# A tuned attention and feed-forward kernel: the differences of the weights' two parts move from VectorE to GpSimd

## The chip, the cores and the metric

The kernel runs on one core of a Trainium2 chip. The metric is the device time of one launch in microseconds (us); the kernel before was run three times, and the median counts. A core has five instruction queues that matter here: TensorE (PE in the profile; PEld is its loading of stationary operands), VectorE (DVE), ScalarE (ACT), GpSimd (POOL) and SyncE (SP), which in this kernel issues all DMAs. Each engine works through its own queue in order; semaphores tie the queues together.

## The reference

Four batches of eight heads run a gated recurrence over 768 steps, and its output goes through a feed-forward layer with a squared ReLU:

```
state = alpha[t][:, None] * state + outer(k[t], v[t])      # per batch and head, 48 x 48
y[t]  = q[t] @ state
x     = y, batches and steps as rows, heads side by side   # 3072 x 384
out   = square(maximum(x @ w_in, 0)) @ w_out               # w_in 384 x 2048, w_out 2048 x 384
```

All tensors are fp32 for the reference; the weights arrive as 64-bit floats, which the kernel turns into fp32 itself.

## The kernel before

**Staging.** The recurrence is cut into blocks of 128 steps: 6 per batch, 24 in all. Four blocks make a group of 512 rows, and there are six groups (0 to 5). TensorE works through the feed-forward layer of group after group, and the recurrence of the groups to come is woven between its matmuls. Blocks need ScalarE (logarithm, exponentials, copies from PSUM) and VectorE (scaling of q and k, masks, states).

**Two parts for each operand.** The first matrix in group 0, three quarters of the second in group 0 and half of it in group 1 run as plain fp32 matmuls (`ffn_in` L901, `out_plain` L817). Everywhere else each operand is split: `b` is a rounded upper part of the weight w, `l` the scaled rest of it, and `d` the difference `b - l`; the activations get parts `a`, `l`, `d` in the same way. Three passes of faster matmuls (`b` with `a`, `l` with `l`, `d` with `d`) then replace one plain product. In the layer's first matrix these are `in_x` (passes b and l, L726) and `in_y` (pass d, L737); in the second `out_x` (L826) and `out_y` (L846).

**Making the weights' parts.** w_in and w_out are cut into eight pieces each ("i0" to "i7", "o0" to "o7" below), of 128 partitions by 768 numbers. Each piece goes through four steps: `cast_w` (ScalarE makes `b`, L646), `rest_w` (VectorE makes `w - b`, through `combine`, L641), `scale_w` (ScalarE scales it to `l`, L660, and stores it to DRAM), and `diff_w` (VectorE makes `d = b - l`, through the same helper, so also L641, and stores it to DRAM with `keep`, L651). `prepare` (L675) places the four steps 1.6 units of matmul work apart; the order in which the sixteen pieces come is i1, o6, i0, o7, i2 to i7, o4, o5, o0 to o3. They are made once, between 105 us and 209 us of the span, under the end of group 0 and in group 1. Later groups load `l` and `d` again from DRAM (`pump`, L680, DMA at L684), in the order in which TensorE will use them, as far as the pool of 26 tiles has room.

**Order.** The order on each engine is the order in which the program emits the steps: the list of words in `AT` up to the first full layer, and from there `weave` (L1041), which emits units of matmul work and drops events between them as their due time comes. Nothing is reordered afterwards.

**The queue of GpSimd.** It clears tiles and makes constants in the first 6.2 us of the span. After that it has held only twelve semaphore instructions, one for each pair of blocks: `passed = nc.gpsimd.nop(...)` (L511, L550) waits for a matmul of the recurrence on TensorE, and TensorE waits for it before the second half of that pair's products, `yb` (L394). That is how the program makes TensorE wait for its own earlier matmuls.

**VectorE in the stretch that the change touches.** Beside the steps above it splits the activations of the second matrix (`hl`, L641, and `hd`, L695, out of `ha`, which ScalarE makes at L691) and those of the first (`xl` L641, `xd` L695, out of `xa`), squares and adds (`hid` L641, L750), scales q and k (L299), splits logarithms (L270, L271), makes masks and states (L425, L455, L471, L472), and adds partial outputs (`osb` L838 and L641).

Of the kernel before, what the change touches and what calls it, by code (L numbers as in the profile page):

```python
# [13 lines left out]
ALU = mybir.AluOpType  # L14
# [11 lines left out]
def kernel(  # L26
# [12 lines left out]
    nc = tc.nc  # L39
# [44 lines left out]
    def wt(name, dt=FP32, shape=(KM, DF // NW)):  # L84
        return wt_pool.tile([128, *shape], dt, tag="wt", name=name)
# [553 lines left out]
    def combine(steps):  # L639
        for o, x, op, z in steps:  # L640
            nc.vector.tensor_tensor(out=o, in0=x, in1=z, op=op)  # L641
# [8 lines left out]
    def keep(x, w, p):  # L650
        nc.sync.dma_start(out=kept_parts[x, w, p], in_=words(made[x, w, p]))  # L651
        stored.add((x, w, p))
# [10 lines left out]
    def diff_w(w, p):  # L663
        b, l = here["b", w, p].bitcast(FP32), made["l", w, p].bitcast(FP32)
        d = made["d", w, p] = wt("wd", FP32R, shapes[w])
        cut.add((w, p))
        combine(((d, b, ALU.subtract, l),))
        keep("d", w, p)
        for x in "ld":
            t = made.pop((x, w, p))  # L670
            if w == "i" or p >= NW - AT["k0"] or (x == "l" and p >= NW - AT["k1"]):
                here[x, w, p] = t
        pump()

    def prepare(at, w, p):  # L675
        step = AT["wstep"]
        fs = (cast_w, rest_w, scale_w, diff_w)
        return [(at + i * step, f, (w, p)) for i, f in enumerate(fs)]

    def pump():  # L680
        while todo and todo[0] in stored and len(here) + len(made) + 2 * NW - len(cut) < room[0]:
            key = todo.pop(0)
            here[key] = wt("w" + key[0], FP32R, shapes[key[1]])
            nc.sync.dma_start(out=words(here[key]), in_=kept_parts[key])  # L684
# [476 lines left out]
```

## Time and profile before

| | |
|---|---|
| runs | 528.08, 524.81 and 525.77 us; median 525.77 us |
| the profiled execution | 526.04 us, of which the span is 524.3 us |
| VectorE busy | 363.8 us (69%), 631 instructions |
| ScalarE busy | 314.8 us (60%) |
| GpSimd busy | 5.3 us (1%), 29 instructions |
| granted TensorE clock | 1.00 over the whole span |
| DMA | 102.36 MB, mean 195 GB/s |

The profiled execution is 0.27 us above the median and spends 1.74 us outside its span. The view of groups gives the busy time of a kind of instruction, the mean duration of one, and what ended the engine's idle time before it. The view of waits gives, for each kind of instruction, the total time that its engine stood idle for it and what released it. The chain that ended last is followed back from the last instruction; its rows are a start, a length and what ran. Rows of the timeline are a start, a duration, the engine and line, and what is written from what.

### The profile page before, as it was taken

What the parts mean: (1) busy time and instruction counts of PE and PEld (TensorE: products, weight loads), DVE (VectorE), ACT (ScalarE), POOL (GpSimd) and SP (SyncE); (2) the same over time, 40 slices, a digit from 0 to 9 for tenths busy, and PEclk for the clock granted to TensorE, in tenths of its full rate; (3) what the DMA queues carried; (4) which work ended last, traced back from release to release, by engine and by line L of the source; (5) the groups of instructions that cost most, each with busy time, mean ns of one, the idle gap of its engine ahead of it and who ended that gap; (6) DMA issues with size and microseconds to landing.
All of it is one profiled execution on the core that took longest, in us unless ns stands there. A gap on an engine that the chain in (4) does not pass through costs nothing.

```text
span 524.3 us, 13198 instructions
## 1 busy us (share of the span) xinstructions
PE 510.0 (97%) x5340; PEld 420.3 (80%) x5340; DVE 363.8 (69%) x631; ACT 314.8 (60%) x662; POOL 5.3 (1%) x29
## 2 busy tenths in 40 slices
PE   7899999998999999889999999999999999999997
PEld 5675446668888669768899988899988899988997
DVE  4778979898879579755697465697365485363861
ACT  3668893688899566456963266963265773164620
POOL 4000000000000000000000000000000000000000
PEclk9999999999999999999999999999999999999999
DMA  9989778235689576998885697864674444798201
GB/s 184 203 266 221 206 209 212 44 91 228 211 214 222 141 228 169 278 330 219 200 208 184 207 285 181 220 194 144 222 262 143 159 149 138 252 352 296 78 0 61
DMA packets 139324, 102.36 MB, mean 195 GB/s; under 512 B 109808, under 2 KB 112896, under 8 KB 139264
## 3 DMA queue, kind: packets, MB, share of 16 engines
q1 hardware_dynamic: 139264, 101.52, 67.6%
q8 instruction: 43, 0.70, 0.6%
q14 instruction: 17, 0.14, 0.1%
HBM read 84.17 MB, written 17.33 MB: 194 GB/s over the span
## 4 chain that ended last, share of the span: by engine, by line
PE 76%; ACT 9%; DVE 7%; DMA 4%; SPq 2%; issue 2%; POOLq 0%; DVEq 0%
PE o L801 33%; PE h L718 31%; PE y L394 4%; ACT power L177 2%; DMA a_in<-in_alpha_dram 2%; PE sckv L414 2%; PE T L571 2%; PE sckv L442 2%; SPq L119 1%; DMA wd<-di 1%; DMA v_in<-in_v_dram 1%; DVE w_out L192 1%; DVE w_out L195 1%; ACT r L917 1%; ACT x L609 1%
## 5 line engine op out<-in xcount | busy, mean ns | idle before, releaser
L718 PE MATMUL h<-xd,wd 128*128 128x512 f32 x240 | 66.8, 393 | 3.5 <-ACT ha L691 1.9
L718 PE MATMUL h<-xa,wb 128*128 128x512 f32 x240 | 68.9, 395 | 0.0
L718 PE MATMUL h<-xl,wl 128*128 128x512 f32 x240 | 67.8, 391 | 0.0
L641 DVE TENSOR_TENSOR hid<-h,hid 128x512 f32<-128x512 f32 x40 | 27.5, 689 | 46.2 <-PE h L718 43.4
L735 ACT ACTIVATE h<-h 128x512 f32<-128x512 f32 x40 | 23.3, 582 | 59.1 <-PE h L718 58.9
L609 ACT COPY x<-y 32x256 f32<-32x256 f32 (+2 forms) x132 | 47.2, 365 | 17.6 <-PE y L394 12.8
L801 PE MATMUL o<-wd,hd 128*128 128x384 f32 x304 | 53.8, 334 | 1.4 <-DVE osb L838 1.4
L718 PEld LDWEIGHTS h<-xd,wd 128*128 128x128 f32 x240 | 44.4, 188 | 13.2 <-ACT ha L691 2.3
L801 PE MATMUL o<-wb,ha 128*128 128x384 f32 x160 | 54.2, 338 | 0.0
L801 PEld LDWEIGHTS o<-wd,hd 128*128 128x128 f32 x304 | 52.7, 188 | 1.7 <-DVE osb L838 1.7
L801 PE MATMUL o<-w_out,hid 128*128 128x384 f32 x160 | 53.5, 490 | 0.0
L801 PE MATMUL o<-wl,hl 128*128 128x384 f32 x160 | 53.5, 335 | 0.0
L718 PEld LDWEIGHTS h<-xl,wl 128*128 128x128 f32 x240 | 45.1, 188 | 10.0 <-DVE xl L641 0.3
L718 PEld LDWEIGHTS h<-xa,wb 128*128 128x128 f32 x240 | 44.3, 188 | 9.2
L801 PE MATMUL o<-wb,hx 128*128 128x384 f32 x144 | 48.7, 338 | 0.0
L801 PE MATMUL o<-wl,hx 128*128 128x384 f32 x144 | 48.1, 334 | 0.0
L801 PEld LDWEIGHTS o<-w_out,hid 128*128 128x128 f32 x160 | 29.9, 190 | 19.7
L911 PE MATMUL h<-x,w_in 128*128 128x512 f32 (+1 forms) x120 | 43.6, 513 | 0.5 <-ACT x L609 0.5
L733 ACT ACTIVATE hid<-h 128x512 f32<-128x512 f32 x40 | 24.3, 607 | 29.2 <-PE h L718 29.1
L691 ACT ACTIVATE ha<-hid 128x512 fp32r<-128x512 f32 x40 | 25.5, 636 | 23.8 <-DVE hx L641 12.9
L911 PEld LDWEIGHTS h<-x,w_in 128*128 128x128 f32 x120 | 22.1, 190 | 18.2 <-issue 14.1
L641 DVE TENSOR_TENSOR hl<-hid,ha 128x512 fp32r<-128x512 f32 x40 | 27.4, 686 | 12.0 <-ACT ha L691 12.0
(117 smaller groups left out, 880.0 us busy)
## 6 DMA issues: line engine op xcount, KB each, us to landing
wd<-do SPq DMA_DIRECT2D x36, 384.0 KB, 3.1
wl<-lo SPq DMA_DIRECT2D x34, 384.0 KB, 5.1
wl<-li SPq DMA_DIRECT2D x32, 384.0 KB
wd<-di SPq DMA_DIRECT2D x32, 384.0 KB, 5.1
raw<-in_moe_w_in_dram SPq DMA_DIRECT2D x8, 768.0 KB, 6.2
raw<-in_moe_w_out_dram SPq DMA_DIRECT2D x8, 768.0 KB, 4.8
v_in<-in_v_dram SPq DMA_DIRECT2D x24, 192.0 KB, 4.9
out_dram<-osb SPq DMA_DIRECT2D x24, 192.0 KB, 2.1
```

The costliest lines, as they stand in the source:

```text
L177: nc.scalar.activation(out=power, in_=power, func=AF.Relu, scale=2.0**23, bias=rebias)
L394: ins = nc.tensor.matmul(out=ys[e][64 * half : 64 * half + D + G * e, m % 2, p // 2, t], lhsT=lhsT, rhs=rhs, start=(half, e) not in seen, ...
L414: nc.tensor.matmul(out=ps[e][HALF[h], 0, p, :], lhsT=ks[rows, p, HALF[h]], rhs=qs[rows, p, HALF[h]], start=True, stop=True, skip_group_che ...
L442: nc.tensor.matmul(out=ps[h][64 * e : 64 * (e + 1), 1, p, G:64], lhsT=tile_of("k", n)[HALF[h], 2 * p + e, :], rhs=tiles["v"][n % NV][HALF[ ...
L609: copy(out=x[kk][to : to + m, t : t + 2], in_=blk[n]["y"][e][r : r + m, :, p // 2],)
L641: nc.vector.tensor_tensor(out=o, in0=x, in1=z, op=op)
L691: nc.scalar.activation(out=a, in_=x, func=AF.Copy, scale=NEAR)
L718: nc.tensor.matmul(out=acc["h", j], lhsT=here[w, "i", p][:, kk, jj * 128 : (jj + 1) * 128], rhs=x_parts[x][:, kk], start=start and kk == 0 ...
L733: nc.scalar.activation(out=hid[j], in_=x, func=AF.Copy, scale=E)
L735: nc.scalar.activation(out=x, in_=x, func=AF.Copy, scale=1.0 + E)
L801: nc.tensor.matmul(out=acc[t][:, 0:DM], lhsT=lhs[:, t * C : (t + 1) * C], rhs=rhs, start=start, stop=stop, skip_group_check=True,)
L911: nc.tensor.matmul(out=ps, lhsT=w[:, kk, c0 : c0 + 128], rhs=xT[g][kk][:, cols], start=(kk == 0), stop=(kk == KM - 1),)
```

## The change

One line of `diff_w` changes its engine. The subtraction has the same operands, sizes and types (128 x 768, two fp32 inputs in SBUF, one output in SBUF); it no longer goes through `combine`, so its line becomes L667. The semaphores follow the new engine.

```diff
     def diff_w(w, p):
         b, l = here["b", w, p].bitcast(FP32), made["l", w, p].bitcast(FP32)
         d = made["d", w, p] = wt("wd", FP32R, shapes[w])
         cut.add((w, p))
-        combine(((d, b, ALU.subtract, l),))
+        nc.gpsimd.tensor_tensor(out=d, in0=b, in1=l, op=ALU.subtract)
         keep("d", w, p)
```

The built program shows what moves: sixteen TensorTensor instructions leave VectorE's queue and stand in GpSimd's, behind its constants and between its semaphore instructions; the order of everything else on TensorE, VectorE, ScalarE and SyncE is the same. In GpSimd's queue the pieces stand between the semaphore instructions as: i1, o6, i0, the fourth semaphore instruction, o7, i2 to i7, the fifth, o4, o5, o0, o1, the sixth, o2, o3.

## The prediction

> **What bounds the kernel now.** I read the page first. TensorE is busy almost throughout, so work taken off VectorE pays only where TensorE stands idle.
>
> ```profile
> span 524.3 us, 13198 instructions
> PE 510.0 (97%) x5340; PEld 420.3 (80%) x5340; DVE 363.8 (69%) x631; ACT 314.8 (60%) x662; POOL 5.3 (1%) x29
> ```
>
> The view of the wd tiles gives what is moved: sixteen subtractions of 0.95 us between 115.7 and 207.2 us. They are the only rows that change their engine.
>
> ```profile
> L641 DVE TENSOR_TENSOR wd<-wb,wl x16: 949/951/959, 115.7 to 207.2; 128x768 fp32r<-128x768 f32 x16
> ```
>
> Then the view of waits, for TensorE alone (us in total, times, longest). Those after 104 us are these three; the idle rest lies ahead of 50 us and in the last 4 us, out of reach of the change.
>
> ```profile
> PE h L718 <- ACT ha L691: 1.9, 1, 1.9
> PE h L718 <- DMA wd<-di: 1.6, 1, 1.6
> PE o L801 <- DVE osb L838: 1.4, 1, 1.4
> ```
>
> The busy time by stretch (us, PE, PEld, DVE, ACT, POOL) says where VectorE matters: from 104 to 126 us VectorE (20.15 of 22) and ScalarE are as full as TensorE; from 128 to 215 us TensorE is never idle and VectorE has 15 us free.
>
> ```profile
> 104.00:126.00 22.00, 20.64 (x290) 14.94 (x289) 20.15 (x33) 19.43 (x41) 0.00 (x0) 1.00 0.50 166
> 128.00:215.00 87.00, 87.00 (x1050) 69.72 (x1049) 71.98 (x128) 65.10 (x137) 0.00 (x0) 1.00 0.73 202
> ```
>
> The chain that ended last shows which subtractions lie on the path in the first stretch (start, length, what):
>
> ```profile
> 115.77 0.87 DVE wd L641
> 116.63 0.87 DVE wl L641
> 117.50 0.61 DVE hl L641
> 118.12 0.02 issue
> 118.14 0.69 DVE hd L695
> 118.83 0.88 DVE wl L641
> 119.73 0.85 ACT wl L660
> ...
> 123.66 0.87 DVE wd L641
> 124.53 0.87 DVE wl L641
> 125.40 0.48 DVE osb L838
> ```
>
> Two of sixteen. The other fourteen run beside TensorE's work.
>
> **Part 1: what VectorE gains.** Each subtraction holds VectorE for 0.87 us from start to start; sixteen make 13.9 us, of which almost all was covered. At 115.77 the piece i1 goes, but hl behind it waits for ha on ScalarE, which ends at 116.55 + 0.61 = 117.16: hl starts at 117.2 and not 117.42, a gain of 0.2 us. The same 0.2 us is handed to wl at 119.73 and along ScalarE's queue, which runs without a gap from there (osb, wb, ha, 4.35 us of copies of x, wl, xa) until xa ends at 129.0. At 123.66 the piece o7 goes: osb L838 could start 0.9 us earlier, near 124.5 when TensorE's last sums are done, and out_y with it. But the matmuls of group 1 behind out_y need xa and xl, and xl follows xa, which came only 0.2 us earlier. So 1.36 us of idle time at 125.9 mostly comes back as a wait for xl, and the gain is 0.2 to 0.4 us; I take 0.3.
>
> **Part 2: what one subtraction costs GpSimd.** The rows of before hold no two-operand instruction on GpSimd. The nearest are a memset and a cast of 128x128 (start, duration):
>
> ```profile
> 2.85 0.20 POOL masks.py:197 MEMSET ident<- 128x128 f32 x1
> 4.00 0.29 POOL L217 CAST causal_r<-causal 128x128 fp32r<-128x128 f32 x1
> ```
>
> With memsets of 128x256 at 310 ns a memset costs 106 ns for each further 128 numbers. At that slope the cast grows to 0.29 + 5 x 0.106 = 0.82 us for 768 numbers, and that is the lower end; six whole casts, 1.73 us, are the upper one. A second operand has to be read as well, so I take 1.7 us, near the upper row. The Trainium skill gives 4,497 ns for such an operation on 2048 numbers ("GPSIMD Engine Reference", 3.1), by proportion an estimate of 1.69 us; no row here shows it.
>
> **Part 3: are the differences late?** On GpSimd they wait only for l from ScalarE (L660), no longer for VectorE's queue. i6 has its l at 153.87 + 0.84 = 154.7, so it ends near 156.4; VectorE ended it at 159.94, and TensorE uses it at 163.96. i7: l at 161.7, end 163.4, used after 166.2. o6 and o7 end near 118.3 and 122.3, wanted at 125.9. All have 2.8 us to spare or more, so a length of 1.7 us costs nothing. The DMAs that store d follow on SyncE, in their old places; SyncE waited 25 us in all for them, with loads behind, and none of those loads kept an engine waiting before 215 us. ScalarE's wb and VectorE's wl now wait for earlier GpSimd pieces at eight places, always one finished 5 us before. In GpSimd's queue o7, o4 and o2 stand behind semaphore instructions that wait for TensorE; of these only o4 meets one that is late (l at 169.1, the recurrence's matmuls done at 170.9), and it still ends at 172.6, against 172.85 on VectorE.
>
> **Part 4: the hold.** GpSimd and VectorE now read SBUF operands at the same time, which no row of before shows. The nearest rows are VectorE's own: a cast of 128x384 (L270) takes 0.35 us, a two-operand product of the same size (L299) 0.55. Reading is what its two-operand instructions are short of, so if GpSimd's reads come out of the same supply, the two hold each other up. At the one end that costs nothing; at the other each piece stops one VectorE instruction for 1.7 us. I take one hold for each piece that meets a waiting hl or xl, with VectorE passing first between its own back-to-back instructions:
> o6 (l ready at 116.64) runs to 118.3, hl starts there and not at 117.42, and wl and ScalarE's queue come 0.9 us later; xa begins at 128.24. i2 (l ready at 128.33) runs to 130.0, holds the first xl from 128.9, and the third xl ends at 131.9 and not 129.9. TensorE's group 1 starts 2.0 us later, and this includes part 1.
> The Trainium skill makes a rule of it: a VectorE instruction with two SBUF inputs and a GpSimd one that reads SBUF share a read interface, and whichever comes second is blocked for the whole instruction ("SBUF — State Buffer", Who interferes with whom). By the rule the sum is the slower one, without it the faster one below.
> Between 128 and 215 us VectorE sheds 11 x 0.87 = 9.6 us and is held for at most 11 x 1.7 = 18.7 us; with its 15 us free the load fits, and only a late release of a PSUM bank or of k and q before a transpose can show: 0 to 1.5 us, taken as 0.3.
>
> **Part 5: the reload at 222 us.** The stores of o2 and o3 (SyncE, 207.33) open a stretch in which the DMA engines are full (0.98 from 215 to 232 us), and the loads of d in it are what TensorE waits for: 1.6 us at 222.4 for di0; the 1.9 us at 229.35, put down to ha, end with the load of di1 that was issued at 219.91, for the matmuls wait for it too. l of o2 and o3 is ready at 203.3 and 204.1, but VectorE reached them only at 206.35, behind masks and states. On GpSimd they end at 205.1 and 206.8 if nothing holds them: the second store goes 1.4 us earlier, and the two waits of 3.5 us shrink by up to as much. With hd of 203.95 meeting GpSimd I take half, 0.7 us.
>
> **Sum**, against the profiled execution of 526.04 us: + 2.0 + 0.3 - 0.7 = + 1.6, so 527.6; that execution lies 0.27 us over the median, so 527.4 us.
>
> **The rivals.**
> *No hold.* The engines do not disturb each other: -0.3 and -1.4, so 525.77 - 1.7 = 524.1 us. For it: no row shows a hold. Against it: VectorE's 0.35 and 0.55 us.
> *GpSimd wins every gap.* A piece that is ready slips in at each dependent pair, too. i1 (l ready 108.87) holds hl at 109.69 for 1.7 us, 0.66 of it idle anyway: 1.0. o6 0.9. i0 goes between hl and hd: 1.7. o7 stops hl at 123: 0.8. i2 1.2. Together 5.6, with 1.0 us of bank stalls behind and no gain at 222 us, since hd goes after o2: 525.77 + 6.6 - 0.3 = 532.1 us, slower by more than 1%. It decides once the holds on the path pass 5.3 us in sum.
> *The semaphore queue.* Behind i0 on GpSimd stands the semaphore instruction that TensorE's yb waits for; yb started at 120.85. If that instruction goes only when i0 is finished, and i0 is held by hd and wl until 120.5, it comes at 122.2. The copies of x on ScalarE wait for yb: with its 0.7 us they start at 122.9, not 122.23 + 0.9, so ScalarE hides it, but out_x behind yb is 1.4 us late and out_y with it: + 1.4 on top, 528.8 us. For it: a queue works in order. Against it: i0 may end at 120.1.
>
> **How the numbers follow.** Forecast 0.45, no hold 0.26, every gap 0.19, the semaphore queue 0.10. A measurement of this kernel can tell about 1%, 5.3 us, from no change. Forecast, no hold and semaphore queue all lie within it; every gap lies above; 0.01 is left for faster, since TensorE's idle time within reach is under 5 us. The forecast's own range is 525.5 to 529.5. The range goes down to 523.8, 0.3 us under no hold, for a subtraction nearer to 0.82 us that lets the reload start earlier still, and up to 531.5, which leaves out most of every gap.
>
> **What would show it.** Sixteen rows on L667 of 1.4 to 2.0 us. VectorE's hl, hd and xl beside them longer than 0.69 us or starting after a piece ends (hold), or at 0.69 as before (no hold). The first matmul of group 1, at 128.8 before, near 130.8. yb right after i0's end would show the semaphore queue. The waits for di0 and di1 at 222 and 229 us shorter in sum than 3.5. The forecast is wrong if a wait for POOL appears on TensorE's L718 or L801, or if pieces take over 3 us each.

## The result

The changed kernel takes 532.22 us (median of 4 runs, 532.05 to 533.45), the kernel before 525.29 us (median of 4, 524.73 to 528.08): a ratio of 1.0124 with a 95% interval of 1.0094 to 1.0154. It is slower by some 6.5 us by that ratio (6.9 us between the medians), above the forecast of 527.4 us and above the end of the range at 531.5 us; the rival in which GpSimd wins every gap had 532.1 us. The profiled execution of after took 532.26 us, at a granted clock of 1.00.

The page of after, for the two lines that were shown of before:

```profile
span 530.5 us, 13220 instructions
PE 513.6 (97%) x5340; PEld 420.1 (79%) x5340; DVE 367.7 (69%) x615; ACT 315.2 (59%) x662; POOL 37.6 (7%) x45
```

VectorE lost sixteen instructions, and it is busy for 3.9 us longer than before. Matched one by one between the two traces, the instructions that stayed grew by 17.4 us in sum, 1.1 us for each piece; nearly all of it lies in thirteen of them, which grew by 0.8 to 1.6 us each. GpSimd is busy for 32.3 us more.

The view of the wd tiles gives the moved rows, now on GpSimd (durations in ns: least, median, most):

```profile
L667 POOL TENSOR_TENSOR wd<-wb,wl x16: 1830/1867/2496, 108.5 to 213.3; 128x768 fp32r<-128x768 f32 x16
```

The view of waits for TensorE (us in total, times, longest), the rows in the reach of the change:

```profile
PE h L718 <- ACT ha L691: 1.7, 1, 1.7
PE o L801 <- ACT wl L660: 1.3, 1, 1.3
PE cs L284 <- DVE lo L271: 1.2, 1, 1.2
...
PE o L801 <- DVE osb L838: 0.7, 1, 0.7
PE T L571 <- DVE k_in L299: 0.6, 1, 0.6
PE o L801 <- ACT osb L824: 0.5, 1, 0.5
...
PE cs L283 <- DVE hi L270: 0.5, 1, 0.5
PE h L718 <- DVE xl L641: 0.4, 1, 0.4
PE o L801 <- DVE hl L641: 0.4, 1, 0.4
```

No row names GpSimd: no difference is late. Instead there are waits for VectorE and for ScalarE's steps behind it, and one of the two waits at the reload, that for di0, is gone.

The busy time by stretch (us, PE, PEld, DVE, ACT, POOL), at the two places shown of before:

```profile
104.00:126.00 22.00, 19.77 (x281) 13.35 (x279) 18.55 (x24) 16.13 (x33) 8.42 (x4) 1.00 0.47 154
128.00:215.00 87.00, 83.76 (x957) 63.92 (x957) 69.29 (x105) 62.47 (x129) 23.23 (x12) 1.00 0.66 179
```

TensorE was busy for 20.64 us of the first and for all of the second; it now stands idle for 2.2 and 3.2 us. VectorE's instructions have a mean of 0.77 us (18.55 / 24) for 0.61, and of 0.66 us for 0.56: it does fewer of them and saves little time.

The chain that ended last runs through the held instructions (start, length, what):

```profile
108.40 0.96 DVE w_out L195
109.36 2.23 DVE hl L641
...
117.66 1.92 DVE hl L641
119.57 0.02 issue
119.60 2.22 DVE hd L695
121.81 0.88 DVE wl L641
...
129.59 0.85 ACT wl L660
130.44 0.53 ACT xa L691
130.97 0.02 issue
130.99 3.13 DVE xl L641 x3
134.12 0.04 issue
134.16 1.89 PE h L718 x7
```

Before, hl and hd on this chain took 0.61 and 0.69 us. The row of the first hl in the timeline of before (start, duration, row):

```profile
109.69 0.69 DVE L641 TENSOR_TENSOR hl<-hid,ha 128x512 fp32r<-128x512 f32 x1
```

To see what runs beside these instructions, here is the timeline of after, GpSimd first and then VectorE (in square brackets, the engine's idle time before the row and what ended it):

```profile
108.53 2.50 POOL L667 TENSOR_TENSOR wd<-wb,wl 128x768 fp32r<-128x768 f32 x1 [102.34 <-ACT wl L660]
117.18 4.08 POOL L667 TENSOR_TENSOR wd<-wb,wl 128x768 fp32r<-128x768 f32 x2 [6.15 <-ACT wl L660]
```

```profile
108.40 0.96 DVE L195 TENSOR_TENSOR w_out<-w_out,power 128x768 f32<-128x768 f32 x1
109.27 2.31 DVE L641 TENSOR_TENSOR hl<-hid,ha 128x512 fp32r<-128x512 f32 x1
...
117.66 1.91 DVE L641 TENSOR_TENSOR hl<-hid,ha 128x512 fp32r<-128x512 f32 x1 [0.56 <-ACT ha L691]
119.60 2.22 DVE L695 SCALAR_TENSOR_TENSOR hd<-ha,hl 128x512 fp32r<-128x512 f32 x1
```

The row of GpSimd's i1 begins at 108.53, while L195 runs: the piece is admitted, which means that it has all it waits for and stands at the head of its queue. It ends at 111.03. Less 1.83 us, the least of the sixteen durations, it began to work at 109.20, when L195 came to its end. hl stood in VectorE's queue right behind L195 and had nothing left to wait for, yet it ends at 111.58, 0.55 us after the piece. So GpSimd got in between two back-to-back instructions of VectorE, and 1.62 of the 1.83 us of its work show up as a longer hl. At 119.6 the same happens between hl and the hd that depends on it (i0, the second of the pair of pieces).

**Where the 6.2 us of span came from.** The timelines of the kernels are cut at the same instructions: S1 from the first hl (109.69 before) to the first matmul of group 1 with xd; S2 and S3 from there to two transposes of k (163.36 and 194.08); S4 on to the first matmul of group 2 (216.49); S5 the reload, to the next transposes (232.27); S6 to the start of the last matmuls with xd (485.24). Lengths in us:

| kernel | S1 | S2 | S3 | S4 | S5 | S6 |
|---|---|---|---|---|---|---|
| before | 23.37 | 30.30 | 30.72 | 22.41 | 15.78 | 252.97 |
| after | 27.99 | 32.19 | 32.44 | 22.99 | 13.74 | 252.83 |
| after less before | +4.62 | +1.89 | +1.72 | +0.58 | -2.04 | -0.14 |

The sum is +6.6; the first hl came 0.4 us earlier in after, a start that differs between executions of one kernel, too (109.69 and 110.81 us in two executions of the kernel before). Each part has its own place, so each can be tried alone.

### The profile page after: what moved, and what is told of

Read it like the earlier page. It is cut to its first block, busy times and chain, and to the rows that moved or that the text cites. A ratio compares the mean times of both kernels' runs of the same rounds, so it can differ in the third digit from the quotient of the medians.

```text
span 530.5 us, 13220 instructions
## 1 busy us (share of the span) xinstructions
PE 513.6 (97%) x5340; PEld 420.1 (79%) x5340; DVE 367.7 (69%) x615; ACT 315.2 (59%) x662; POOL 37.6 (7%) x45
## 4 chain that ended last, share of the span: by engine, by line
PE 78%; DVE 11%; ACT 5%; issue 2%; DMA 2%; SPq 1%; DVEq 0%; POOLq 0%; ACTq 0%
PE o L801 30%; PE h L718 29%; PE h L911 7%; PE y L394 3%; PE T L571 2%; PE sckv L414 2%; ACT x L609 2%; PE sckv L442 2%; DVE hl L641 1%; DVE wl L641 1%; DVE hd L695 1%; DMA v_in<-in_v_dram 1%; SPq L119 1%; DVE w_out L195 1%; DVE w_out L192 1%
## 5 line engine op out<-in xcount | busy, mean ns | idle before, releaser
L667 POOL TENSOR_TENSOR wd<-wb,wl 128x768 fp32r<-128x768 f32 x16 | 32.2, 2020 | 177.2 <-ACT wl L660 164.4
L641 DVE TENSOR_TENSOR hl<-hid,ha 128x512 fp32r<-128x512 f32 x40 | 31.6, 791 | 13.6 <-ACT ha L691 13.6
L691 ACT ACTIVATE ha<-hid 128x512 fp32r<-128x512 f32 x40 | 25.5, 637 | 23.8 <-DVE hx L641 12.9
```

Of the source, the lines that this page charges most:

```text
L667: nc.gpsimd.tensor_tensor(out=d, in0=b, in1=l, op=ALU.subtract)
L691: nc.scalar.activation(out=a, in_=x, func=AF.Copy, scale=NEAR)
```

## The experiments

The theory: an instruction of VectorE with two SBUF operands and a GpSimd instruction that reads SBUF exclude each other, GpSimd gets in whenever VectorE passes from one instruction to the next, and each piece stops VectorE until it is done. The Trainium skill has the first half of this as a rule ("SBUF — State Buffer", Who interferes with whom), and the rows above agree with it (2.31 us for 0.69). The rivals: GpSimd's mere activity or its writes slow VectorE; or the pieces come late; or the loss lies in the DMAs behind.

**The two halves: first5 and other11.** first5 leaves on GpSimd only the five pieces of S1:

```diff
-        combine(((d, b, ALU.subtract, l),))
+        engine = nc.gpsimd if (w, p) in (("i", 1), ("o", 6), ("i", 0), ("o", 7), ("i", 2)) else nc.vector
+        engine.tensor_tensor(out=d, in0=b, in1=l, op=ALU.subtract)
```

> Only i1, o6, i0, o7 and i2 run on GpSimd; the other eleven differences stay on VectorE. Hold theory (a GpSimd subtraction stops the next VectorE instruction with two SBUF operands until it is done): the whole delay of the first stretch comes back, 4.6 us at the first matmul with xd, and nothing is regained at 222 us, so about 525.3 + 4.6 = 529.9 us (528.5 to 531). VectorE's hl, hd and xl show rows of about 2 us beside these five pieces. Lateness theory (TensorE or its semaphore instruction waits for GpSimd): none of these pieces is late for TensorE, so 525.3 us within 1 us, unless yb is late.

other11 is its complement (`not in`):

> The complement: i1, o6, i0, o7 and i2 stay on VectorE, the other eleven run on GpSimd. Hold theory: no delay up to the first matmul with xd (133.1 us as before), then 4.2 us of stalls up to the first matmul of group 2 and 2.0 us regained at the reload behind it: about 527.5 us (526.5 to 528.5); the two parts of the change add up. Lateness theory: i6, i7 or o4 are late and a wait for POOL shows on TensorE, 530 us or more.

| kernel | S1 | S2 | S3 | S4 | S5 | median us | ratio, 95% interval |
|---|---|---|---|---|---|---|---|
| first5 | 27.97 | 30.30 | 30.73 | 22.39 | 14.97 | 530.83 | 1.0056, 1.0028 to 1.0084 |
| other11 | 23.38 | 32.20 | 32.46 | 23.00 | 13.84 | 529.45 | 1.0038, 1.0014 to 1.0063 |

The kernel before had 526.41 us beside them. Each half changes its own stretches by the amount that it has in the full change, and no other, but for S5, where both are shorter. So first5's expectation that nothing is regained at the reload was wrong: with the stores of o2 and o3 in their old places it has 0.8 us there, its wait for di 0.9 us instead of 1.6. The gains of the two halves, 0.8 and 1.9 us, make more than the 2.0 us of the full change. The earlier stores are therefore not the only thing that shortens S5, and what each contributes in the full change stays open.

Of the 4.2 us of S2 to S4, the view of waits of other11 shows 2.2 us as TensorE's idle time, in the same three waits as after (for lo 1.2, hi 0.5 and k_in 0.5 us). Idle time is counted there from the modelled end of the matmul before. Counted by the starts of TensorE's matmuls, matched one by one with those of before, 3.8 of the 4.2 us arise in four places: 1.0 us at the first hi and lo, 0.9 at the transposes of k and q, 1.4 at the second lo, and 0.5 at the products `sckv` (L414) behind the held hd. At each of them VectorE had been held shortly before. Two of these holds in the timeline of after, of rows that took 0.55 and 0.56 us before (start, duration, row):

```profile
167.20 2.19 DVE L299 TENSOR_TENSOR k_in<-k_in,inv 128x384 f32<-128x384 f32 x1
...
194.25 2.06 DVE L271 TENSOR_TENSOR lo<-a_in,hi 128x384 fp32r<-128x384 f32 x1
```

In the times the two halves cost 2.9 and 2.0 us by the ratios, 4.4 and 3.0 us by the medians; 529.45 us for other11 lies above the 526.5 to 528.5 us that were expected. The executions scatter (523.9 to 531.9 us for the kernel before) with the granted clock, whose mean over the span lies between 0.987 and 1.00 in them. Those of at least 0.999 alone, a choice made afterwards, have medians of 530.16 us for first5, 527.99 for other11 and 525.78 for before: +4.4 and +2.2, together 6.6 us. The full change, whose four executions were all at 1.00, lies 6.4 us above the same 525.78 and 6.9 above the 525.29 beside it.

**Activity without reading: extra_memset.** The subtractions stay on VectorE as before, and GpSimd writes instead of reading, twelve memsets at the moment at which a piece would run:

```diff
+        for i in range(12):
+            clear = nc.gpsimd.memset(causal, 0.0)
+            if i == 0:
+                dep(clear, scaled_at[w, p])
```

> The kernel before, with all subtractions on VectorE; in addition GpSimd clears an unused 128x128 tile twelve times, from the moment at which each piece's l is ready, so that it is active and writes SBUF for 1.8 us or more beside the same VectorE instructions, without reading. Hold theory (by reads): 525.3 us within 1 us, and hl, hd, xl keep 0.69 us. If any GpSimd work beside VectorE holds it: 529 us or more.

The ratio was 1.0024 (0.9991 to 1.0058). The timeline, GpSimd's memsets and then VectorE's hl and hd in the middle of them:

```profile
117.05 9.38 POOL L672 MEMSET causal<- 128x128 f32 x36 [4.76 <-ACT wl L661]
```

```profile
117.71 0.68 DVE L641 TENSOR_TENSOR hl<-hid,ha 128x512 fp32r<-128x512 f32 x1
118.43 0.69 DVE L702 SCALAR_TENSOR_TENSOR hd<-ha,hl 128x512 fp32r<-128x512 f32 x1
```

Nothing is held under 9.38 us of writes: it takes reads. The kernel has another loss, which was not meant: the memsets of one piece take 3.1 us instead of 1.8, so the semaphore instruction behind them came late, and TensorE's yb waited for it. In the view of waits:

```profile
PE y L394 <- POOLq L511: 1.9, 1, 1.9
```

S1 grew by 1.36 us by that. It is the semaphore queue of the prediction, brought about by a longer GpSimd queue; in after itself it cost nothing. S5 grew as well, to 17.14 us from 15.78, with the waits for di and ha hardly shorter than before (1.4 and 1.9 us) but a granted clock of 0.50 for 3.4 us from 231.87 us on; more of that below.

**One operand read: copy_only.** GpSimd copies l and leaves out the subtraction and its second operand:

```diff
-        combine(((d, b, ALU.subtract, l),))
+        nc.gpsimd.tensor_copy(out=d, in_=l)
```

> All sixteen pieces on GpSimd, but as a copy of l to d, one operand read in place of two: the subtraction is left out. Hold theory by any SBUF read of GpSimd: rows near 0.9 us (0.82 by the slope of the memsets), hl and hd beside them 1.3 to 1.6 us, and the first matmul with xd 24.5 to 25.5 us after the first hl. If only a GpSimd instruction with two operands stands in VectorE's way: hl, hd, xl keep 0.69 us and the stretch 23.4 us.

One execution took 525.74 us. The timeline, GpSimd's first two copies, then the two hl beside them:

```profile
109.84 1.53 POOL L667 CAST wd<-wl 128x768 fp32r<-128x768 f32 x1 [103.64 <-ACT wl L660]
117.62 0.83 POOL L667 CAST wd<-wl 128x768 fp32r<-128x768 f32 x1 [6.25 <-ACT wl L660]
```

```profile
110.61 1.31 DVE L641 TENSOR_TENSOR hl<-hid,ha 128x512 fp32r<-128x512 f32 x1
...
118.12 0.88 DVE L641 TENSOR_TENSOR hl<-hid,ha 128x512 fp32r<-128x512 f32 x1 [0.56 <-ACT ha L691]
```

A copy takes 0.83 us where nothing is in its way, and it holds VectorE, but for less: hl grows by 0.62 and 0.19 us, S1 by 0.78 us (24.15 for 23.37), S2 to S4 by 0.13 us. S5 is 13.73 us, as short as in after. The expectation had 24.5 to 25.5 us for S1 and 1.3 to 1.6 us for each hl and hd; it holds for the first hl alone, for the copy beside the second had begun 0.5 us ahead of it. One operand read is enough for a hold, and the shorter instruction gives the shorter hold.

**The same work in smaller instructions: split3.** All sixteen on GpSimd, each in three parts of 128x256:

```diff
+        for c in range(3):
+            part = slice(c * 256, (c + 1) * 256)
+            nc.gpsimd.tensor_tensor(
+                out=flat(d)[:, part], in0=flat(b)[:, part], in1=flat(l)[:, part], op=ALU.subtract
+            )
```

> All sixteen pieces on GpSimd, each as three subtractions of 128x256. Hold theory, with a hold that lasts for one GpSimd instruction and is passed on at each boundary to whoever waits: a held VectorE instruction waits for one third, 0.6 us, and not for 1.7 us; the first stretch loses about 2.5 to 3 us and not 4.6 (first matmul with xd 25.5 to 26.5 us after the first hl, 27.99 in the changed kernel), in all 528 to 530 us. If GpSimd keeps the operands from third to third, or if the loss comes from the amount read and not from the length of an instruction: 27.9 us or more there and 532 us in all.

The ratio was 1.0055 (1.0026 to 1.0084). The timeline of GpSimd's first piece, and VectorE beside it:

```profile
110.49 3.69 POOL L669 TENSOR_TENSOR wd<-wb,wl 128x256 fp32r<-128x256 f32 x3 [104.31 <-ACT wl L660]
```

```profile
111.24 1.22 DVE L641 TENSOR_TENSOR hl<-hid,ha 128x512 fp32r<-128x512 f32 x1
112.50 1.10 DVE L699 SCALAR_TENSOR_TENSOR hd<-ha,hl 128x512 fp32r<-128x512 f32 x1
```

hl and hd are each held by 0.4 to 0.5 us, for no more than one part, which takes 0.72 us where nothing is in its way, and GpSimd's three parts stretch to 3.69 us (2.09 us undisturbed), since VectorE gets in between them as GpSimd gets in between VectorE's. S1 costs 2.25 us instead of 4.62, S2 to S4 0.6 instead of 4.2; S5 is 15.21 us, so most of the gain at the reload is gone as well. The intervals of the ratios of split3 and of the full change do not overlap. The two engines take turns at the boundaries of instructions; the size of GpSimd's instruction is the price of one turn.

**The gain at the reload: last2, last2_split, last2_again.** last2 moves o2 and o3 alone, whose stores open the full stretch of the DMA engines:

> Only o2 and o3 run on GpSimd. Hold theory with the reload: one VectorE instruction (hd) is held for 1.5 us where TensorE has work, the second store of d goes about 1 us earlier, and the waits for di0 and di1 shrink by up to 2.0 us: 523.3 to 524.8 us, faster than before. If the gain at 222 us in the changed kernel came from TensorE being late and not from the earlier stores: 525.3 us.

S4 cost 0.56 us (22.97), as in after, by the one hd of 2.15 us that meets them. TensorE's idle time at the reload fell from 3.50 to 2.42 us, but S5 took 16.31 us instead of less, and the ratio was 0.9973 (0.9943 to 1.0003): 526.0 us, not the 523.3 to 524.8 that were expected, and no gain that can be told from none. last2_split cuts the two pieces into thirds as above, to keep the gain without the hold:

> Only o2 and o3 on GpSimd, each as three subtractions of 128x256. If the hold lasts for one GpSimd instruction: hd is held for 0.6 us and not for 1.5, the 0.56 us lost before group 2 shrink to 0.2 or less, and the gain of the earlier stores at the reload stays, 1.1 us or more less idle time on TensorE: 524 to 525 us against 525.3, the fastest of all. If thirds change nothing: as with o2 and o3 whole, 0.997 of before.

The hold's cost was gone (S4 22.41), the gain too: six parts took 5.09 us, o3 ended 8.0 us ahead of group 2 instead of 9.3, and S5 was 16.50 us at an undisturbed clock, with 4.22 us of idle time. The ratio was 1.0013 (0.9977 to 1.0048), at 526.0 us and not the 524 to 525 us that were expected. last2 was then run again:

> The differences of o2 and o3 alone go to GpSimd, as in last2, timed again in more rounds since the interval there held no change and its profile had a granted clock of 0.90 around the reload. By the hold theory with the earlier end of o3: the stretch up to group 2 costs 0.5 to 0.6 us (hd held by 1.5 us), the reload's idle time is 2.4 us against 3.5 and its stretch, at an undisturbed clock, is 13.8 us against 15.8, so 1.2 to 1.5 us faster than before: a ratio of 0.997 to 0.998. Its rival, that the shorter idle time at the reload is given back behind it (a clock that falls when TensorE waits less): the stretch from the reload on is again 16 us with a granted clock of 0.90, and the ratio is 1.000 to 1.001.

The ratio was 1.0001 (0.9981 to 1.0021). The busy time by stretch of last2_again, around the reload (PEclk, DMA share and GB/s stand last):

```profile
228.00:230.00 2.00, 0.59 (x3) 0.17 (x1) 2.00 (x6) 1.97 (x4) 0.00 (x0) 1.00 1.03 413
230.00:232.00 2.00, 1.61 (x7) 1.32 (x8) 1.79 (x3) 0.18 (x1) 0.00 (x0) 0.94 1.08 351
232.00:234.00 2.00, 2.00 (x6) 1.57 (x5) 0.00 (x0) 0.56 (x2) 0.00 (x0) 0.50 0.81 161
234.00:236.00 2.00, 2.00 (x35) 1.32 (x33) 1.28 (x3) 1.04 (x3) 0.00 (x0) 0.71 0.82 250
```

TensorE's granted clock falls to 0.50 some 1.4 us after its wait has ended (0.2 us after it in last2), and in this profile that eats what the shorter wait brings: the idle time from 222 us on is 2.4 us, as the theory has it, and the time is not better, as its rival has it. The profile of last2 has the same dip (0.51 from 232 to 234 us), those of before and after have none. But extra_memset has it too, and there the stores of d have not moved and the waits at the reload are hardly shorter; other11 and copy_only have shorter waits than last2 (1.8 and 1.7 us) and no dip. So a shorter wait is neither needed for the dip nor enough for it. Why the clock falls stays open.

Executions at a clock of at least 0.999 have medians of 525.01 us (5 of 10) and 524.72 us (5 of 12) against 525.78 and 525.22 us of before, 0.8 and 0.5 us faster; last2_split has 525.86 us (6 of 10) against 524.84, 1.0 us slower. Over all executions no gain can be told from none. These kernels, and first5, also spend 1.9 to 2.1 us outside their span where before spends 1.7 to 1.8; no view shows why, and it takes 0.2 to 0.3 us off any gain.

The kernel before, run once more as before_again for its stretches, gave S1 to S5 within 0.03 us of the first execution, with the same two waits of 1.9 and 1.6 us at the reload, in 527.11 us. The waits are steady. What was expected:

> The kernel before once more, for a second trace of the reload: if the two waits of TensorE there (3.5 us in sum) are steady, 3.3 to 3.7 us again; if they vary from run to run by more than 0.8 us, what the experiments gain at the reload is partly chance.

## Why the prediction was wrong

**The price of a piece (part 2): right.** A piece takes 1.83 to 1.87 us where nothing is in its way (1.7 was taken); a copy takes 0.83 us, where the slope of the memsets had given 0.82. Part 1's gain of 0.3 us can't be checked by itself: every run that takes a subtraction off this stretch of VectorE lets GpSimd read there.

**Part 3: right.** TensorE waits for no row on L667. (SyncE's waits for the differences before were 30.2 us in sum and not 25, which changes nothing in the argument.)

**Part 4, the hold: right in kind, wrong in the step "VectorE passing first between its own back-to-back instructions".** It is the step that failed. GpSimd passes at every such boundary. For S1, read from the starts on the chain, counted from the start of the first hl in each trace: i1 costs 0.9 us (the second hl at 113.94, where 113.06 would be the old distance), o6 1.0 (the third hl ends 1.9 later by the same count), i0 1.5 (its hd ends 3.4 later), o7 0.1 (the fourth hl starts 3.4 and ends 3.5 later), i2 1.1 (the last xl ends 4.6 later): 4.6 us, and not 2.0. The forecast had charged only o6 and i2 and had let i1 and i0 wait for free. first5 shows this term alone (+4.60).

**The same part's term for 128 to 215 us was mis-sized: 0.3 was taken, with 0 to 1.5 us as bounds, and 4.2 us came.** The working compared sums, 18.7 us of holds with 24.6 us of room. But the room is not where the holds fall: TensorE takes up the lo and the k_in that were stopped (2.06 us for 0.56, 2.19 for 0.55) as soon as they are done, and VectorE's free time lies elsewhere. In TensorE's waits 2.2 us of it appear (lo, k_in, and a hi that is not held itself). other11 shows the term alone.

**Part 5: right in direction, small in size.** -0.7 was taken, and -1.4 for earlier stores alone; -2.0 came. o3 ends 9.3 us ahead of group 2 instead of 8.3, and the wait for di0 disappears. That the gain passes 1.4 us fits first5, which has 0.8 us without earlier stores: the step took the stores to be the only cause.

**The sum** is therefore +4.6 + 4.2 - 2.0 = +6.8 us (6.6 with the -0.14 of S6) for +2.0 + 0.3 - 0.7 = +1.6 us.

**The rivals.** No hold fell with the first row of 2.31 us. The semaphore queue did not come about in after, although yb starts at 121.26 us, just as i0 ends, which was to be its sign. The fourth semaphore instruction went at 118.91, as i0 behind o6 was admitted (its row begins at 118.98) and not when it was finished. yb follows the start of TensorE's previous matmul by 0.27 us, exactly as in before, and in first5 it starts at 121.20, ahead of i0's end at 121.23. extra_memset shows that the mechanism exists. GpSimd wins every gap was the right mechanism with nearly the right time, 532.1 for 532.2 us, but in part by terms that cancel: 5.6 us in S1 where 4.6 came (o7 cost 0.1 and not 0.8), 1.0 us behind where 4.2 came, and no gain at the reload where 2.0 came. It had a chance of 0.19 and lay outside the range, whose upper end was set to leave it out.

## What to carry to other kernels

Work moved to GpSimd is not free for VectorE, even where GpSimd is idle and nobody waits for its result: an instruction there that reads SBUF can stop VectorE's next instruction with two SBUF operands for nearly its whole length (here up to 1.6 us of 1.83), so count the holds one by one where the engine behind VectorE waits, and not as a sum against free time. Where such work has to go there, small instructions cost less (2.3 us instead of 4.6 in the tight stretch), and where VectorE had one operand in PSUM it was not held. A rival whose mechanism the rows can't exclude belongs inside the range.

## What the runs showed of the hardware

GpSimd won the boundary between two back-to-back instructions of VectorE (i1, i0), and VectorE won that between two of GpSimd's (hl between o6 and i0, and the thirds of split3). Each time the winner had been waiting while the other engine worked, so first come, first served would give the same; no run here tells it from a fixed order. The profile gives the hold as a longer row of the instruction that is held (2.31 us for 0.69), and GpSimd's own wait as a longer row of its piece (2.50 us for 1.83); neither is shown as idle time.

VectorE with one operand in PSUM is not held. In the timeline of after, GpSimd's piece and VectorE's instructions beside it:

```profile
159.03 1.85 POOL L667 TENSOR_TENSOR wd<-wb,wl 128x768 fp32r<-128x768 f32 x1 [2.64 <-ACT wl L660]
```

```profile
158.66 0.34 DVE L455 TENSOR_TENSOR us<-sckv,s 128x192 f32<-128x192 f32 x1
159.04 0.36 DVE L471 TENSOR_TENSOR s<-sckv,us 128x192 f32<-128x192 f32 x1
159.43 1.66 DVE L472 TENSOR_TENSOR s<-s,last 128x192 f32<-128x192 f32 x1
```

`s<-sckv,us` runs in 0.36 us inside the piece; `s<-s,last`, of the same size but with both operands in SBUF, takes 1.66 us where it took 0.36 before.

A semaphore instruction in GpSimd's queue goes when the instruction ahead of it is admitted: at 118.91 us, while o6 ran until 119.01 and i0's row went from 118.98 to 121.26.
